# Two blocks of a feed-forward layer multiplied jointly by Strassen's products, and two attention blocks moved together, in a planned attention and feed-forward kernel

## The chip, the cores and the metric

The kernel runs on one core of a Trainium2 chip. The metric is device time in microseconds (us), the median of repeated executions. Engines are named as in the profile: PE (TensorE matmul), PEld (its weight loads), DVE (VectorE), ACT (ScalarE), POOL (GpSimd), SP (the queue that issues the DMAs).

## The reference

Kernelized attention, then a squared-ReLU feed-forward layer, then a normalized gated one, all in float32:

```python
def phi(x):                       # q, k: [4, 8, 576, 64], omega: [128, 64]
    proj = np.einsum('bhsd,md->bhsm', x, omega)
    h = proj - np.sum(x * x, axis=-1, keepdims=True) / 2.0
    return np.exp(h - np.max(h, axis=-1, keepdims=True)) / np.sqrt(m)
kv = np.einsum('bhsm,bhsd->bhmd', phi(k_s), v)
num = np.einsum('bhsm,bhmd->bhsd', phi(q_s), kv)
attn = num / (np.einsum('bhsm,bhm->bhs', phi(q_s), z)[..., None] + 1e-06)
...
h = np.maximum(x @ w_in, 0.0)     # x: [2304, 512], w_in: [512, 2048]
y = h * h @ w_out                 # w_out: [2048, 512]
...
xn = y / np.sqrt(np.mean(y * y, axis=-1, keepdims=True) + 1e-06) * rms_g
g = xn @ w_gate                   # w_gate, w_val: [512, 1536]
out = (g / (1 + np.exp(-g))) * (xn @ w_val) @ w_out2
```

## The kernel before

The 2304 tokens are cut into five blocks: block 0 to 3 hold 512 tokens of one batch element each, and a fifth, REM, holds the last 64 tokens of all four (256 columns). All matmuls of the two feed-forward layers are split in precision: each float32 operand becomes a high part (an ACT cast) and a low part (a DVE or POOL subtraction, helper `split`, L398), and a product is three matmuls (high by high, high by low, low by high), so that four 128-row pieces of the model dimension make 12 matmuls of 128x512.

`attention(b)` (L519) treats four pairs of heads of a block. A pair visits PE in small groups: features of k and of q (L577, 8 matmuls each), key-value sums (L635, L638), transposes (L686), numerators (L692, L697), transposes back (L722, L732). Between them DVE takes maxima and quotients and ACT the exponentials (L596). For block 2 and 3 (`long`) some of these groups are merged.

`moe1(j)` (L758) is the first feed-forward layer for one block: 16 chunks of 128 hidden units; `hpart` (L791, L804) makes a chunk's hidden tile h with 12 matmuls into a PSUM bank of class h, ACT takes the ReLU (L818) and the square (L820), and `ypart` (L826, L834) adds the chunk into four accumulators of class acc with another 12. Block 0 decodes the weights from their stored format and keeps part of them in SBUF (`wu`); the rest is written to DRAM and read again by each later block (`wr`). The second layer, `moe2` (L1126), takes blocks 0 and 1 together, then 2 and 3, and already uses seven products for eight (`seven`, L1057): for two chunks and two blocks 7 products of 6 matmuls, with DVE sums between them; its weight combinations are made beside the first layer by `make_units` (L918).

Nothing of this runs in the written order. Every operation becomes a node with an engine, a duration, a priority and its dependencies; `Plan.run` (L113) plays them through with those durations and buffer counts, and the order in which they start there is the order in which the instructions are issued, engine by engine. On the chip each engine then takes its instructions strictly in that order. The PSUM banks are divided by class: t (attention and others), h and acc, 2, 2 and 4 of eight. Early on, when PE has nothing to do in the plan, `fill` (L105) puts filler matmuls (L480, two of 128x256 on ones, into a spare bank) in its place, up to the planned time `FILL[1]`.

The calls before: `attention(0)`, then `attention(b + 1)` and `moe1(b)` for b = 0 to 3, so that attention 1 stands beside block 0, attention 2 beside block 1 and attention 3 beside block 2; then REM and `moe2` twice.

Of the kernel before, what the change touches and what calls it, by code (L numbers as in the profile page):

```python
# [9 lines left out]
F32 = mybir.dt.float32  # L10
# [28 lines left out]
class Node:  # L39
    __slots__ = ("eng", "dur", "fn", "prio", "idx", "tail", "alts", "deps", "ndeps", "outs", "bufs", "acq")  # L40


class Plan:
# [12 lines left out]
    FILL = (0.6, 45.0, 0.21)  # L56
# [11 lines left out]
    def add(self, eng, dur, prio, fn, r=(), w=(), after=(), tail=0.0, pre=(), alts=()):  # L68
        n = Node()
        n.alts = [(eng, dur, fn), *alts]  # L70
# [34 lines left out]
    def fill(self):  # L105
        n = Node()
        n.eng, n.dur, n.tail, n.prio, n.idx = "PE", self.FILL[2], 0.0, 0.0, -1
        n.bufs, n.acq, n.outs, n.deps, n.alts = [], [], [], set(), []
        b, f = self.filler
        n.fn = lambda: f(b.ap)  # L110
        return n

    def run(self):  # L113
# [15 lines left out]
        seq = 0  # L129

# [32 lines left out]
        while done < len(self.nodes):  # L163
# [4 lines left out]
            while events and events[0][0] <= now + 1e-9:  # L168
                _, _, kind, n = heapq.heappop(events)
                if kind == 0:  # L170
                    i = pick_alt(n)
                    heapq.heappush(ready[n.alts[i][0]], (n.prio, n.idx, i, n))
# [17 lines left out]
            for e in engs:  # L190
                if busy[e] > now + 1e-9:
                    continue
                held = []
                pick = None
                blocked = set()
                while ready[e]:
                    item = heapq.heappop(ready[e])
# [12 lines left out]
                    if ok:  # L210
                        for b, c, s in got:
                            slot[b] = (c, s)
                        pick = n
                        n.eng, n.dur, n.fn = n.alts[item[2]]
                        break
                    for b, c, s in got:
                        self.free[c].insert(0, s)
                    held.append(item)
                for it in held:
                    heapq.heappush(ready[e], it)  # L220
# [3 lines left out]
                if pick is not None:  # L224
# [3 lines left out]
                    if isinstance(pick.dur, Shared):  # L228
                        start = max(now, busy["POOL"])
                        held_by["DVE"] = start + pick.dur  # L230
                    busy[e] = start + pick.dur * (2.0 if e == "PE" and now < self.COLD else 1.0)
# [16 lines left out]
def kernel(  # L248
# [36 lines left out]
    LONG = 2  # L285
    SCALE = float(D) ** -0.25
# [9 lines left out]
    ph1_stack, att_stack = ExitStack(), ExitStack()  # L296
# [39 lines left out]
    plan.alloc["sm"] = slot_alloc("att", "sm", [P, 16], F32)  # L336
    plan.alloc["xa"] = slot_alloc("w2a", "xa", [P, 512], F32R)
# [18 lines left out]
    w1_d = [tc.dram_tile([P, 2, 512], F32, name=f"w1d{i}") for i in range(2 * C1)]  # L356

# [7 lines left out]
    b_w1d = [Buf(ap=t) for t in w1_d]  # L365

# [16 lines left out]
    def dma(prio, outap, inap, nbytes, r=(), w=(), after=()):  # L383
        return plan.add(
            "SP", nbytes / 311e3, prio,
            lambda: nc.sync.dma_start(out=outap(), in_=inap()), r, w, after, tail=2.0,
# [132 lines left out]
    def attention(b):  # L519
        base = (b - 1) * float(C1) if b else -25.0  # L520
        step = 3.7 if b else 6.0
        lead = base - (6.0 if b else 2.85)
        long = b >= LONG
        rem_x, rem_p = [], []
        ssr = Buf(["sm"])
# [8 lines left out]
        def operand(ldp, src, cls):  # L534

            x = Buf(["lt", cls])
            dma(ldp, lambda: x.ap, src, 262144, w=[x])
            return x

        def rem_prep(pr0):  # L540
            rem_x[:] = [operand(lead, lambda: rest_t[b].rearrange("p h n -> p (h n)"), "tr")]
            xr = Buf(["ld"], view=lambda t: t.rearrange("p h r d -> p (h r) d"))
            dma(lead, lambda: xr.ap, lambda: rest_r[b], 262144, w=[xr])
            row_norms(pr0, xr, ssr)
            dma(lead, lambda: vr_t[P - SR:], lambda: rest_v[b], 133120, w=[b_vr])

        def pair(hp):
# [7 lines left out]
            ld = pb - 3.0  # L555
            dma(ld + 0.1, lambda: vt, lambda: v_r[b, hp], 266240, w=[bv])
            stats = {}

            def transposed(nm, p0):
# [4 lines left out]
                dma(ld + 0.05, lambda: x.ap, lambda: src[b, hp].rearrange("p h r d -> p (h r) d"), 262144, w=[x])  # L564
# [3 lines left out]
            def features(p0, pbuf, x, places, ss, after=()):  # L568
# [10 lines left out]
                head = plan.add("PE", 0.24 * R + 0.2, p0, mm, [x, b_oms], fps, after, pre=[pbuf])  # L579
                mx = Buf(["sm"])  # L580
                for h, fp in enumerate(fps):
                    js = slice(*places[h])
                    plan.add("DVE", dve(M * R), p0 + 0.25 * u * h,
# [22 lines left out]
            features(pb + u, pk, xk, ODD, stats["k"], list(last_q))  # L606
# [5 lines left out]
            xq = transposed("q", pb + 2 * u)  # L612
            last_q[:] = [features(pb + 4 * u, pq, xq, ODD, stats["q"])]
# [17 lines left out]
            for h in range(2):  # L631
# [9 lines left out]
                if not long:  # L641
                    plan.add("PE", 0.13 * 5, pb + 3 * u + h * u, kv, [pk, pr, bv, b_vr, b_vz], [(kvp, h)],
                             kv_free)
            if long:
                plan.add("PE", 0.13 * 10 + 0.4, pb + 4 * u, kv2, [pk, pr, bv, b_vr, b_vz, b_const], [kvp], kv_free,
                         pre=[qrt])
# [5 lines left out]
            for hl in range(2):  # L652
                b_x[b, hl, hp] = Buf(["x"])
            xh, xl = b_x[b, 0, hp], b_x[b, 1, hp]
# [45 lines left out]
            for hs in ([(0, 1)] if long else [(0,), (1,)]):  # L700
# [9 lines left out]
                plan.add("PE", 0.44 * len(hs), pb + (6 + h0_) * u, trs, [pq] + [b_const],  # L710
                         [qps[h] for h in hs], pre=[qts[h] for h in hs])
                for h in hs:
                    copy(pb + (6.2 + h) * u, lambda h=h: qts[h].ap, lambda h=h: qps[h].ap, 512, [qps[h]], [qts[h]])
                plan.add("PE", 0.13 * R * len(hs) + (0 if h0_ else 0.36), pb + (7 + h1_) * u, mms,
                         [bkv] + [qts[h] for h in hs] + ([] if h0_ else [qrt]), [nps[h] for h in hs],
                         pre=[] if h0_ else [xw])
# [13 lines left out]
            def xtr():  # L730
# [27 lines left out]
    def moe1(j):  # L758
# [525 lines left out]
```

## Time and profile before

| what | value |
|---|---|
| median of 3 runs | 970.8 us (969.86 to 972.18) |
| profiled execution, its own time | 972.6 us |
| span, first to last instruction | 970.8 us |
| PE busy | 955.1 us (98%) |
| DVE, ACT, POOL busy | 688.4, 518.6, 78.8 us |
| granted TensorE clock, mean | 0.998 |

Span and busy times are those of the profiled execution. A matmul's record is longer than the step from one start to the next, since matmuls overlap; starts, not durations, give its cost. Matmuls on float32 tiles of the attention appear as two records each.

### The profile page before, as it was taken

What the parts mean: (1) busy time and instruction counts of PE and PEld (TensorE: products, weight loads), DVE (VectorE), ACT (ScalarE), POOL (GpSimd) and SP (SyncE); (2) the same over time, 40 slices, a digit from 0 to 9 for tenths busy, and PEclk for the clock granted to TensorE, in tenths of its full rate; (3) what the DMA queues carried; (4) which work ended last, traced back from release to release, by engine and by line L of the source; (5) the groups of instructions that cost most, each with busy time, mean ns of one, the idle gap of its engine ahead of it and who ended that gap; (6) DMA issues with size and microseconds to landing.
All of it is one profiled execution on the core that took longest, in us unless ns stands there. A gap on an engine that the chain in (4) does not pass through costs nothing.

```text
span 970.8 us, 16150 instructions
## 1 busy us (share of the span) xinstructions
PE 955.1 (98%) x6036; PEld 793.0 (82%) x6036; DVE 688.4 (71%) x1241; ACT 518.6 (53%) x1078; POOL 78.8 (8%) x69
## 2 busy tenths in 40 slices
PE   8999999999999999999999999999999999999998
PEld 7877777787888788788889888888878888888886
DVE  5889988756747556645745889989897757577573
ACT  6987788656446446445645658554443452323220
POOL 1123312000101010000100110000000000000000
PEclk9999999999999999999999999999999999999999
DMA  7878788888678565598978444324233221222203
GB/s 248 271 255 285 245 283 310 284 305 293 223 238 284 185 222 176 181 309 280 317 254 316 127 142 124 105 88 133 87 107 131 77 76 33 77 61 59 70 29 108
DMA packets 74845, 179.45 MB, mean 185 GB/s; under 512 B 8848, under 2 KB 12048, under 8 KB 74768
## 3 DMA queue, kind: packets, MB, share of 16 engines
q1 hardware_dynamic: 74768, 178.43, 56.0%
q8 instruction: 47, 0.77, 0.3%
q14 instruction: 30, 0.25, 0.1%
HBM read 143.27 MB, written 35.13 MB: 184 GB/s over the span
## 4 chain that ended last, share of the span: by engine, by line
PE 82%; DVE 8%; DMA 4%; ACT 3%; issue 1%; POOL 1%; SPq 0%; POOLq 0%; DVEq 0%; ACTq 0%
PE h L804 17%; PE acc L834 17%; PE acc L1046 12%; PE t L1107 11%; PE h L1046 11%; PE t L1046 4%; PE t L577 3%; DMA st<-in_w_gate_dram 1%; DMA ld<-in_k_r_dram 1%; PE t L692 1%; PE t L635 1%; DVE cc L1066 1%; PE acc L480 1%; PE t L686 1%; PE h L1107 1%
## 5 line engine op out<-in xcount | busy, mean ns | idle before, releaser
L834 PE MATMUL acc<-g,wr 128*128 128x512 f32 (+1 forms) x660 | 151.5, 373 | 1.2 <-POOL g L392 1.2
L804 PE MATMUL h<-x,wr 128*128 128x512 f32 x528 | 134.6, 398 | 0.0
L834 PEld LDWEIGHTS acc<-g,wr 128*128 128x128 f32 x660 | 113.4, 189 | 22.2 <-POOL g L392 1.4
L401 ACT CAST wq<-wq 128x512 fp32r<-128x512 f32 x108 | 66.5, 619 | 103.2 <-DMA wq<-w2d4g 15.8
L1107 PE MATMUL t<-wq,ub 128*128 128x512 f32 x474 | 116.7, 391 | 1.4 <-DVE oa L1115 1.3
L804 PEld LDWEIGHTS h<-x,wr 128*128 128x128 f32 x528 | 97.6, 189 | 21.7
L1046 PE MATMUL acc<-x,wq 128*128 128x512 f32 x324 | 106.9, 389 | 0.0
L1107 PEld LDWEIGHTS t<-wq,ub 128*128 128x128 f32 x474 | 88.4, 188 | 22.2 <-DVE oa L1115 2.9
L392 DVE TENSOR_TENSOR wq<-wq 128x512 fp32r<-128x512 f32 x108 | 79.7, 745 | 30.4 <-ACT wq L401 30.0
L818 ACT ACTIVATE f<-h 128x512 f32<-128x512 f32 (+1 forms) x80 | 44.9, 562 | 90.1 <-PE h L804 90.1
L1046 PE MATMUL h<-x,wq 128*128 128x512 f32 x252 | 85.3, 390 | 0.0
L392 DVE TENSOR_TENSOR g<-f,g 128x512 fp32r<-128x512 f32 (+1 forms) x61 | 39.6, 650 | 45.6 <-ACT f L499 34.5
L1046 PEld LDWEIGHTS acc<-x,wq 128*128 128x128 f32 x324 | 60.8, 188 | 12.8 <-DVE cc L1066 0.2
L1046 PE MATMUL acc<-xa,wq 128*128 128x512 f32 x192 | 69.8, 389 | 0.0
L834 PE MATMUL acc<-g,wu 128*128 128x512 f32 (+1 forms) x300 | 68.3, 373 | 0.0
L1066 DVE TENSOR_TENSOR cc<-acc,cc 128x512 f32<-128x512 f32 x84 | 57.8, 688 | 14.3 <-PE acc L1046 13.1
L1115 DVE TENSOR_TENSOR oa<-t,oa 128x512 f32<-128x512 f32 x75 | 50.9, 688 | 21.8 <-PE t L1107 21.3
L596 ACT ACTIVATE p<-t,sm 128x128 f32<-128x128 f32 x212 | 57.8, 382 | 14.2 <-DVE sm L589 12.2
L439 ACT ACTIVATE dw<-st 128x512 f32<-128x512 f32 x68 | 46.4, 692 | 29.2 <-DMA st<-in_w_out_dram 8.7
L804 PE MATMUL h<-x,wu 128*128 128x512 f32 x240 | 61.5, 399 | 0.0
L1046 PE MATMUL h<-xa,wq 128*128 128x512 f32 x168 | 60.5, 389 | 0.0
L834 PEld LDWEIGHTS acc<-g,wu 128*128 128x128 f32 x300 | 51.7, 189 | 9.6
(213 smaller groups left out, 1641.5 us busy)
## 6 DMA issues: line engine op xcount, KB each, us to landing
wr<-w1d SPq DMA_DIRECT2D x88, 512.0 KB, 4.6
st<-in_w_out_dram SPq DMA_DIRECT2D x28, 512.0 KB, 4.9
w1d<-wr SPq DMA_DIRECT2D x22, 512.0 KB, 4.3
st<-in_w_in_dram SPq DMA_DIRECT2D x16, 512.0 KB, 4.5
st<-in_w_gate_dram SPq DMA_DIRECT2D x12, 512.0 KB, 5.5
st<-in_w_val_dram SPq DMA_DIRECT2D x12, 512.0 KB, 5.2
st<-y SPq DMA_DIRECT2D x23, 256.0 KB, 4.2
v<-in_v_r_dram SPq DMA_DIRECT2D x16, 260.0 KB, 4.2
```

Source lines behind the costliest of these rows:

```text
L392: return lambda: en.tensor_tensor(out=lo(), in0=src(), in1=f32(hi()), op=ALU.subtract)
L401: first = plan.add("ACT", act(n), prio, lambda: nc.scalar.copy(out=hi(), in_=src()), rd, [whi], after, pre=[blo] if blo is not bhi else [])
L439: lambda: nc.scalar.activation(out=out(), in_=hf(), func=AF.Abs, scale=65536.0), [(st, 1)], [w])
L577: nc.tensor.matmul(fps[h].ap[:, i, :], lhsT=x.ap[ps, c], rhs=oms[ps, :], start=True, stop=True)
L596: nc.scalar.activation(out=pbuf.ap[:, j, :], in_=fp.ap[:, i, :], func=AF.Exp, bias=mx.ap[:, j:j + 1])
L804: nc.tensor.matmul(hb.ap[:, :n], lhsT=u.ap[:, wl, kk * P:(kk + 1) * P], rhs=xcols(j, xl, kk)(), start=(gi == 0 and ii == 0), stop=(gi == l ...
L818: lambda: nc.scalar.activation(out=rb.ap[:, :n], in_=hb.ap[:, :n], func=AF.Relu), [hb], [rb])
L834: nc.tensor.matmul(accs[e].ap[:, :n], lhsT=u.ap[:, w, es], rhs=x.ap[:, :n], start=(c == 0 and i == 0), stop=(c == C1 - 1 and i == 2))
L1046: nc.tensor.matmul(bank.ap[:, cols], lhsT=u.ap[:, wl, c0 + kk * P:c0 + (kk + 1) * P], rhs=x[kk][xl].ap[:, :cols.stop - cols.start], start= ...
L1066: lambda: nc.vector.tensor_tensor(out=out.ap, in0=bank.ap, in1=x.ap, op=ALU.add), [bank, x], [out])
L1107: nc.tensor.matmul(o.ap, lhsT=x[xl].ap[:, c0:c0 + P], rhs=us[f"o{i}"].ap[:, wl, :], start=i == n == 0, stop=i == 1 and n == 2)
L1115: lambda: nc.vector.tensor_tensor(out=oa.ap, in0=o.ap, in1=oa.ap, op=ALU.add), [o, oa], [oa])
```

## The change

Block 2 and 3 go through the first layer together (`moe1_pair`): the 16 chunks form eight pairs (c, c + 8). With `ALONE = 4`, pairs 0 to 3 are multiplied for block 2 alone, pairs 4 to 7 for both blocks by `seven`, then pairs 0 to 3 for block 3 alone; four of the eight pairs are joint. Attention 2 and 3 both stand beside block 1. New are: combinations of the raw weights (`sums`, to DRAM and back), combinations of the attention's results (`operands_pair`, with x of block 3 kept in DRAM), a third bank of class t for one of class h, priorities and planner constants, and a cost for changing between kinds of matmul in the planner.

```diff
-    FILL = (0.6, 45.0, 0.21)
+    SWITCH = 0.11
+    NEAR = 3.12
+    FILL = (0.6, 51.22, 0.21)
...
+                line = sorted(ready[e], key=lambda it: (it[0] - self.NEAR * (e == "PE" and mode > 0 and it[3].mode == mode), it[1]))
...
+    ALONE = 4
+    GATE = 8
+    PAIR = 2
+    HC = C1 // 2
+    ATT = ((-30.46, 5.32, 1.52), (-0.43, 3.33, 11.54), (C1 + -2.86, 1.49, 9.4), (C1 + 1.82, 1.29, 2.25))
...
-        "t": 2, "h": 2, "acc": 4,
+        "t": 3, "h": 1, "acc": 4,
...
-        base = (b - 1) * float(C1) if b else -25.0
-        step = 3.7 if b else 6.0
-        lead = base - (6.0 if b else 2.85)
+        base, step, lead = ATT[b]
+        lead = base - lead
...
+    def moe1_pair(ops, room):
...
+        def both(p, c):
+            pos = p - 2.99
+            u0 = unit(pos, c, 0)
+            ux, uy = (summed_unit(pos, c, k) for k in range(2))
+            ua = unit(pos, c + HC, 0, slice(256, 512))
+            w = {"A11": (u0, 0), "A12": (u0, 256), "S2": (ux, 0), "S3": (ux, 256), "S1": (uy, 0), "S4": (uy, 256),
+                 "A22": (ua, 256)}
+            r, nd = seven(p, w, ops, nodes[-2:-1] or [h_all[1, C1 - 1]], ["t", "h"], ["cs"], b_w1p)
+            nodes.append(nd)
+            used((u0, ux, uy, ua), nd)
+            return {k: squared(p + 0.02, r[i], i == 0) for i, k in enumerate(((0, 0), (0, 1), (1, 0), (1, 1)))}
...
+        work = [(c, 0) for c in range(ALONE)] + [(c, None) for c in range(ALONE, HC)] + [(c, 1) for c in range(ALONE)]
...
     attention(0)
-    for b in range(B):
-        if b + 1 < B:
-            attention(b + 1)
-        moe1(b)
...
+    attention(1)
+    moe1(0)
+    for b in range(PAIR, B):
+        attention(b)
+    moe1(1)
...
+    for c in range(ALONE, HC):
+        sums(c, C1 + 2.28 + 0.85 * (c - ALONE))
+    xp = operands_pair(PAIR * C1 + -29.26, ["xs", "x"], ["cs", "gs", "ys"])
+    hp_ = moe1_pair(xp, ["cs", "ys", "gs"])
```

On PE, block 2 before, one hidden tile takes 12 matmuls (x is the attention's result, wr the weights):

```order
L804 MATMUL h_3667<-x_1414,wr_3226 128x512
L804 MATMUL h_3667<-x_1736,wr_3226 128x512
L804 MATMUL h_3667<-x_2067,wr_3226 128x512
L804 MATMUL h_3667<-x_2422,wr_3226 128x512
L804 MATMUL h_3667<-x_1415,wr_3226 128x512
L804 MATMUL h_3667<-x_1737,wr_3226 128x512
L804 MATMUL h_3667<-x_2068,wr_3226 128x512
L804 MATMUL h_3667<-x_2423,wr_3226 128x512
L804 MATMUL h_3667<-x_1414,wr_3226 128x512
L804 MATMUL h_3667<-x_1736,wr_3226 128x512
L804 MATMUL h_3667<-x_2067,wr_3226 128x512
L804 MATMUL h_3667<-x_2422,wr_3226 128x512
```

On PE now, the first joint pair: two of its seven products, 6 matmuls each, into banks of class t (xs are combined operands):

```order
L1144 MATMUL t_4788<-x_2872,wu_1262 128x512
L1144 MATMUL t_4788<-x_3059,wu_1262 128x512
L1144 MATMUL t_4788<-x_2873,wu_1262 128x512
L1144 MATMUL t_4788<-x_3060,wu_1262 128x512
L1144 MATMUL t_4788<-x_2872,wu_1262 128x512
L1144 MATMUL t_4788<-x_3059,wu_1262 128x512
L1144 MATMUL t_4802<-xs_4597,wr_4576 128x512
L1144 MATMUL t_4802<-x_4649,wr_4576 128x512
L1144 MATMUL t_4802<-xs_4598,wr_4576 128x512
L1144 MATMUL t_4802<-x_4650,wr_4576 128x512
L1144 MATMUL t_4802<-xs_4597,wr_4576 128x512
L1144 MATMUL t_4802<-x_4649,wr_4576 128x512
```

Four hidden tiles (two chunks, two blocks) take 42 matmuls where they took 48.

On PE, at the end of attention 0, where the first chunk of block 0 begins, before (L480 are the fillers):

```order
L804 MATMUL h_884<-x_842,wr_767 128x512
L804 MATMUL h_884<-x_843,wr_767 128x512
L804 MATMUL h_884<-x_842,wr_767 128x512
L480 MATMUL acc_180<-ones 128x256 x2
L804 MATMUL h_926<-x_623,wu_894 128x512
L804 MATMUL h_926<-x_624,wu_894 128x512
L804 MATMUL h_926<-x_623,wu_894 128x512
```

The same place now (L501 are the fillers, L746 and L756 the last transposes of attention 0):

```order
L746 MATMUL t_998<-ident,xw_927 64x64 x2
L756 MATMUL acc_1004<-ident,xw_927 128x128 x4
L501 MATMUL acc_197<-ones 128x256 x24
L835 MATMUL h_838<-x_1005,wr_749 128x512
L835 MATMUL h_838<-x_1006,wr_749 128x512
L835 MATMUL h_838<-x_1005,wr_749 128x512
```

There are 102 filler matmuls in all where there were 82, and the last 24 stand in front of the first chunk's last piece.

On PE in block 1, now, numerators, key-value sums and a transpose of one attention stand in one group between matmuls of a chunk:

```order
L835 MATMUL h_4225<-x_2362,wr_3674 128x512
L716 MATMUL t_4234<-kv_83,qt_4163 64x65 x8
L721 MATMUL t_4234<-kv_83,qr_4000 64x65 x2
L716 MATMUL t_4235<-kv_83,qt_4164 64x65 x8
L656 MATMUL t_4258<-v_81,p_4182 64x65 x8
L659 MATMUL t_4258<-vr,pr_3287 64x65 x2
L656 MATMUL t_4258<-v_81,p_4182 64x65 x8
L659 MATMUL t_4258<-vr,pr_3287 64x65 x2
L642 MATMUL t_4258<-ident,pr_3287 128x64 x2
L835 MATMUL h_4225<-x_1403,wr_3674 128x512
```

Before, beside blocks 1 and 2, the numerators (L692) and the key-value sums (L635) stood in groups apart, with feed-forward matmuls between them. Over the whole program the stretches of feed-forward matmuls on PE fall from 83 to 79.

## Rows read from the trace of the kernel before

**Rows 1.** The page: busy time by engine; the chain that ended last, by engine.

```profile
PE 955.1 (98%) x6036; PEld 793.0 (82%) x6036; DVE 688.4 (71%) x1241; ACT 518.6 (53%) x1078; POOL 78.8 (8%) x69
...
PE 82%; DVE 8%; DMA 4%; ACT 3%; issue 1%; POOL 1%; SPq 0%; POOLq 0%; DVEq 0%; ACTq 0%
```

**Rows 2.** Windows by stage: length, busy us (instructions) of each engine, granted clock, DMA.

```profile
0.00:50.80 50.80, 47.70 (x615) 42.26 (x616) 37.87 (x100) 38.57 (x112) 5.90 (x12) 1.00 0.78 265
50.80:187.00 136.20, 131.34 (x965) 103.60 (x966) 117.36 (x234) 108.69 (x236) 32.63 (x23) 0.99 0.82 275
187.00:300.00 113.00, 112.39 (x861) 89.67 (x860) 73.43 (x159) 63.87 (x149) 5.89 (x7) 1.00 0.78 263
300.00:411.00 111.00, 111.00 (x859) 88.88 (x858) 66.36 (x148) 56.46 (x142) 9.00 (x7) 1.00 0.62 208
...
551.60:760.00 208.40, 207.74 (x937) 172.00 (x936) 184.08 (x291) 110.33 (x191) 7.01 (x5) 1.00 0.38 116
...
966.30:970.80 4.50, 0.00 (x0) 0.00 (x0) 0.67 (x1) 0.00 (x0) 0.00 (x0) 0.84 0.53 117
```

**Rows 3.** Who PE waited for: us in total, times, longest us.

```profile
PE t L577 <- ACT p L596: 2.4, 4, 0.8
PE t L1107 <- DVE oa L1115: 1.3, 5, 0.6
...
PE acc L834 <- POOL g L392: 1.2, 1, 1.2
PE t L635 <- ACT p L596: 1.1, 2, 0.9
```

**Rows 4.** PE in order of time, block 1: start us, us, line, tiles, count.

```profile
293.77 2.88 PE L804 MATMUL h<-x,wr 128*128 128x512 f32 x12
296.58 1.16 PE L577 MATMUL t<-oms,tt 64*128 64x128 f32 x16
297.67 3.02 PE L834 MATMUL acc<-g,wr 128*128 128x512 f32 x12
300.53 2.88 PE L804 MATMUL h<-x,wu 128*128 128x512 f32 x12
303.25 2.20 PE L834 MATMUL acc<-g,wr 128*128 128x512 f32 x9
```

**Rows 5.** PE in order of time, the start: fillers, and waits in brackets.

```profile
1.05 2.93 PE L480 MATMUL acc<-ones 128*128 128x256 f32 x12 [1.05 <-DVE ones L464]
...
14.60 2.66 PE L480 MATMUL acc<-ones 128*128 128x256 f32 x20
17.19 0.37 PE L577 MATMUL t<-oms,tt 64*128 64x128 f32 x1
```

**Rows 6.** Windows of 3 us after the last filler; the column before the last two is the clock.

```profile
50.00:53.00 3.00, 2.13 (x15) 1.38 (x13) 2.19 (x6) 2.99 (x7) 1.47 (x1) 1.00 0.93 297
53.00:56.00 3.00, 2.69 (x18) 2.26 (x19) 3.00 (x7) 1.62 (x3) 0.00 (x0) 0.77 0.89 347
56.00:59.00 3.00, 3.00 (x10) 2.32 (x10) 2.15 (x7) 2.32 (x5) 0.00 (x0) 0.66 0.87 271
```

**Rows 7.** DVE and POOL at 107 us, in order of time; DVE's sums of the second layer.

```profile
107.43 0.68 DVE L531 TENSOR_REDUCE sm<-ld 128x8 f32<-128x512 f32 x1
108.02 1.35 DVE L435 SCALAR_TENSOR_TENSOR st<-st 128x512 uint32<-128x512 uint32 x1
...
107.53 1.29 POOL L392 TENSOR_TENSOR wr<-dw,wr 128x512 fp32r<-128x512 f32 x1 [8.16 <-ACT wr L401]
...
L1066 DVE TENSOR_TENSOR cc<-acc,cc 128x512 f32<-128x512 f32 x84 | 57.8, 688 | 14.3 <-PE acc L1046 13.1
```

**Rows 8.** ACT's ReLU of one chunk, and PE around it.

```profile
312.09 0.63 ACT L818 ACTIVATE f<-h 128x512 f32<-128x512 f32 x1
...
310.01 2.20 PE L834 MATMUL acc<-g,wu 128*128 128x512 f32 x9
...
314.04 1.31 PE L804 MATMUL h<-x,wr 128*128 128x512 f32 x5
```

More of the change, by code (lines that the diff above doesn't have):

```diff
@@ L129, in run @@
         seq = 0
+        mode = 0
         def push(t, kind, n):
@@ L365 @@
     b_w1d = [Buf(ap=t) for t in w1_d]
+    b_w1s = {key: Buf(ap=t) for key, t in w1s_d.items()}
+    b_xd = Buf(ap=x_d)
+    raw = {}
     def f32(t):
@@ L385, in dma @@
             "SP", nbytes / 311e3, prio,
-            lambda: nc.sync.dma_start(out=outap(), in_=inap()), r, w, after, tail=2.0,
+            lambda: nc.sync.dma_start(out=outap(), in_=inap()), r, w, after, tail=2.5,
         )
@@ L812, in hpart @@
                 wb = [(u, parts[i][0]) for i, _ in group]
-                h_nodes[c] = plan.add("PE", pe(n, len(group)), base + c, mm, list(dict.fromkeys(wb + xb)), [hb])
+                h_nodes[c] = plan.add("PE", pe(n, len(group)), base + c + 0.2, mm, list(dict.fromkeys(wb + xb)), [hb],
+                                      [h_nodes[c - 1]] if j == REM and c else ())
             h_all[j, c] = h_nodes[c]
@@ L920, in make_units @@
             make_halves(c, ki, pos + ki)
-        for i in range(2):
-            store(pos + 2, (c, f"o{i}"), raw_unit(pos + 2, (w_out2, c + NC2 * i), last[-2:]))
+        for i, w in enumerate(two_raw(pos + 2, (w_out2, c), (w_out2, c + NC2))):
+            store(pos + 2, (c, f"o{i}"), w)
     def read_unit(c, nm, pos, gates):
@@ L938, with sums, part @@
     summed, held = [], []
+    begun = []
+    def sums(c, pos):
+        a, b = (Buf(["st"], view=lambda t: t.rearrange("p n t -> p (n t)").bitcast(F32).rearrange(
+            "p (t n) -> p t n", t=2)) for _ in range(2))
+        gates, begun[:] = begun[:] or last_split[:1], []
+        for t, cc in ((a, c), (b, c + HC)):
+            if kept(cc):
+                u, gate = w1[2 * cc], gates
+            else:
+                u, gate = t, []
+                dma(pos - 1.0, lambda t=t: t.ap, lambda cc=cc: w1_d[2 * cc], 524288, r=[b_w1d[2 * cc]], w=[t],
+                    after=gates)
+            begun.append(plan.add("DVE", Shared(dve(512)), pos, lambda t=t, u=u: nc.vector.tensor_tensor(
+                out=t.ap[:, 1, :], in0=f32(u.ap[:, 0, :]), in1=f32(u.ap[:, 1, :]), op=ALU.add), [u], [t], gate))
+        def part(t, k, i):
+            return lambda: t.ap[:, k, 256 * i:256 * i + 256]
+        for o, i, x, xi, xk, y, yi, yk, op in (
+                (b, 0, b, 0, 1, b, 1, 1, ALU.add),
+                (a, 1, a, 0, 1, b, 0, 1, ALU.subtract),
+                (a, 0, b, 0, 0, a, 0, 1, ALU.subtract),
+                (b, 1, a, 1, 1, a, 0, 0, ALU.subtract)):
+            both_sbuf(pos, part(o, 0, i), part(x, xk, xi), part(y, yk, yi), op, 256, [a, b], [o], False)
+        for k, t in enumerate((a, b)):
+            last.append(dma(pos, lambda k=k: w1s_d[c, k], lambda t=t: t.ap[:, 0, :], 262144, r=[t], w=[b_w1s[c, k]]))
     def rms(j, base, gates, cls, room, keep):
@@ L1055, with seven @@
     BANKS = ["h", "acc"]
-    def seven(prio, kind, us, ops, after):
-        a, b, d = Buf(BANKS), Buf(BANKS), Buf(BANKS)
-        s, u2, u3 = Buf(["cc"]), Buf(["cc"]), Buf(["cc"])
-        w0, w1_, w2_ = us[kind + "0"], us[kind + "1"], us[kind + "2"]
-        k4 = "gv".index(kind)
+    def seven(prio, w, ops, after, banks, cls, opened):
+        a, b, d = Buf(banks), Buf(banks), Buf(banks)
+        s, u2, u3 = Buf(cls), Buf(cls), Buf(cls)
         def plus(bank, x, out):
@@ L1202 @@
     plan.add("NONE", 0.0, 0.0, open_w2b, w=[b_w2b], after=ph1_nodes)
-    sets = [read_units(c, E1 + (c - 1.0 if c else -7.0), held[:2]) for c in range(NC2)]
+    sets = [read_units(c, E1 + (c - 0.48 if c else -1.99), held[:2]) for c in range(NC2)]
     hidden0 = moe2(0, sets, x01, None)
```

293 lines of the change are left out of this document (228 added, 65 removed), and 1 row of the table slots.

## The prediction

> **What bounds the kernel now.** I read the page first. PE is busy 955.1 of 970.8 us, the next engine, DVE, 71% [rows 1]. The chain that ended last is 82% PE [rows 1], and the rest of it lies mostly at the start and beside block 0. The windows by stage say where the missing 15.7 us are [rows 2]: 3.1 in the first 50.8 us, 4.9 from there to 187 us (block 0 with attention 1), 0.6 and 0.0 beside blocks 1 and 2, 4.5 after the last matmul. So from 187 us on PE's own work is the time, and what matters is how many matmuls it has and how far apart they start. The waits that exist are few [rows 3]: for the exponentials p (2.4 and 1.1 us), for the low part of REM's last chunk on POOL (1.2), for the row sums of the second layer (1.3).
>
> The price of a matmul is read from starts [rows 4]: 12 matmuls begin at 300.53 and the next group at 303.25, so 2.72 us or 0.227 each. The same rows show what an attention group costs beyond itself: the 12 ahead of the features take 2.81 (293.77 to 296.58) and the 12 behind them 2.86 (297.67 to 300.53), 0.23 us in all more than 2.72 each.
>
> **The change, part by part.**
>
> Products. A joint pair has 42 matmuls where it had 48. The loop makes four pairs joint (pairs 4 to 7), so 24 matmuls of 128x512 go, which the order confirms: 5028 without fillers before, 5004 now. 24 by 0.227 is **5.4 us off** the engine that sets the time.
>
> Attention groups. 83 stretches of feed-forward matmuls become 79; four interruptions by 0.23 [rows 4] are **0.9 us off**. The attention's own matmuls are the same.
>
> The start. 20 more fillers, two of them among the first 14, which run slow (12 in 2.93 us, 0.24 each), the others at 2.59 us for 20 (14.60 to 17.19), 0.13 each [rows 5]: 18 by 0.13 and 2 by 0.24 are 2.8 us. Fillers cost nothing if PE would have waited there anyway, and 2.8 if it wouldn't. By the order the useful work ahead of the last filler is the same in both (80 key-value, 72 numerator and 32 transpose matmuls in each; 9 feed-forward matmuls fewer, one group of features and a few transposes more), so I take **2.8 us on**. Against it: behind the last filler of before, from 50 to 56 us, PE idles 0.87 + 0.31 us, and the granted clock falls from 2.4 to 1.2 GHz for a while (means 0.77 and 0.66 over 53 to 59 us), which costs 3 by 0.23 and 3 by 0.34, 1.7 us [rows 6]. Now 24 fillers stand exactly there, so PE is not idle before the first long stretch: I take **1.2 and 1.7 us off**. The start comes out even, with 0 to -2.9 if the fillers fill what was waiting, and +2.8 if the fall of the clock and the idling only move.
>
> The Trainium skill, "TensorE: Matmul & The Clock Gate", section "What's actually happening", says that the low clock is the default and that activity releases it; by that rule steady fillers keep the 1.7 us. Rows 6 agree as far as they go: the fall comes right after the row in which PE is busy least. If fillers did not count as activity, the 1.7 us would stay in the time.
>
> DVE, ACT, POOL. By the order DVE has 98 more instructions (1243 to 1341), ACT 13, POOL 13, mostly 128x512. At DVE's 0.69 us [rows 7] that is 68 us. It lies beside PE: the blocks 1 to REM (187 to 551.6 us) hold 220 us of DVE work in 365 us now, and would hold 288 in about 358, or 80%. Beside the second layer DVE is busy 184.1 of 208.4 us, 88%, and PE misses 0.7 us there [rows 2], with the same `seven`. So this is **nothing**, as long as no stage goes above what that one shows. The joint stretch is the densest: I count 124 DVE instructions by 364 matmuls, some 77 us in 83, 93%. If the cover is gone there, the price is what PE saves in that stretch, 5.4 us.
>
> The Trainium skill, "SBUF — State Buffer", section "SBUF: two separate sides", says that DVE with two SBUF inputs and a POOL instruction shut each other out for a whole instruction. Rows 7 agree: at 108.02 a DVE instruction takes 1.35 us beside POOL's. By that rule each of 13 more POOL instructions can cost DVE about 0.7 us, 9 us in all, which PE would see only where DVE is the bound.
>
> DMA and SP. 523 issues become 542. 13 reads of 512 KB go, and three half reads, 8 stores and 8 loads of combined weights, 5 reads for the sums and x of block 3 come; the bytes are about the same, and block 0 (share 0.82 [rows 2]) loses none and gains next to none. Nothing.
>
> One bank of class h instead of two. A chunk's first matmul now waits until the ReLU of the chunk before has read the bank. In the latest case I found, h ends by 310.2 us, ACT is done at 312.72, and the next h begins at 314.04 [rows 8]; the accumulation between them, 12 by 0.227, always covers 2.72 us of it. So nothing, and at most some tenths of a us where ACT is late. The third bank of class t goes the other way: the features (two banks each) wait for the exponentials that still hold t, 3.5 us in all [rows 3], and could stop waiting. Between 0 and 3.5 off I take 0, since the attention pairs now come faster.
>
> Two attentions beside block 1. The stage of block 1 has 384 matmuls of the layer (16 chunks by 24), 87 us by 0.227; of its 113 us [rows 2] the other 26 are attention 2. With attention 3 it would be 139 us. By the order I count 100 us of DVE work there, 72%, less than the 117.4 of 136.2 us beside block 0 [rows 2]. The wait that could come is the third rival.
>
> Sum: -5.4 - 0.9 + 2.8 - 1.2 - 1.7 = -6.4 us against the execution's own 972.6, or 966.2. That execution was 1.8 us above the median of 970.8, so the median after is **964.5 us**.
>
> **The rivals.**
>
> *The start keeps its loss.* The fillers delay PE, and idling and the low clock come a little later all the same: +2.9, 967.4 us. For it: the planner sets fillers by planned, not real, idleness. Against: the gap they now stand in is the real one.
>
> *The third bank frees the features.* The 3.5 us of waits for p [rows 3] go as well: 961.0 us. For it: nearly all waits of the middle are of this one kind. Against: ACT and DVE beside block 0 are at 80% and 86% [rows 2], and a bank doesn't make them faster.
>
> *The joint stretch is bound by DVE.* The 5.4 us are saved on PE and waited for DVE: 969.9 us, no change that can be measured. From: DVE above 82 us in that stretch; POOL's collisions [rows 7] work towards it. Against: 88% with no wait in the second layer.
>
> *Slower: attention waits beside block 1.* Attention 1 beside block 0 makes PE wait 4.9 us for four pairs [rows 2], 1.2 per pair, nearly all for exponentials and features. With a pair of heads every 17 us (139 by 8) instead of 28 (113 by 4), the eight pairs of attention 2 and 3 could wait as much: 9.7, less the 0.6 that blocks 1 and 2 wait now, is +9.1, or 973.6 us. It decides from 6.3 by 8, about 0.8 us per pair. For it: the pairs follow closely and PE takes its instructions in order. Against: what makes block 0 wait is the decoding of the weights on DVE and ACT, which is not there in block 1.
>
> **How the numbers follow.** 0.2% (1.9 us) is about what a measurement of this kernel can tell from no change. The forecast gets 0.43, the start 0.15, the third bank 0.16, DVE 0.13, the waits 0.13. The first three are faster by over 0.2% (0.74), DVE is the same (0.13), the waits are slower (0.13). The range goes from 957.5 (the third bank's 961.0 with the start's -2.9 and a little more) to 972.5, which leaves out the worse part of the waits and what nobody foresees; the forecast's own range is 961 to 968.
>
> **What would show it.** Products: 24 matmuls fewer, and the joint pairs at 0.227 us per matmul with no wait inside `seven`. Start: a clock of 1.00 and less than 0.5 us of idle time on PE from 50 to 60 us, and about 1.2 + 1.7 us less lost there than the fillers add. Waits: PE's idle time beside block 1 under 2 us. DVE: under 90% in the joint stretch. The prediction is wrong if PE idles more than 6 us between 187 us and the second layer, or if matmuls there start farther apart than 0.227 us.

## The result, and the profile after

The changed kernel takes 960.4 us (median of 4 runs, 958.6 to 961.7) beside 971.5 for the kernel before: ratio 0.9886, 95% interval 0.9863 to 0.9909, or 11.1 us less. The forecast was 6.3 less (964.5). Sign and range (957.5 to 972.5) hold; the size does not, and the time lies just outside the 961 to 968 that the forecast gave itself. The profiled execution took 961.7 us, span 959.8.

The page's busy times and the chain by engine, as in [rows 1]:

```profile
PE 946.5 (99%) x6032; PEld 787.8 (82%) x6032; DVE 734.7 (77%) x1339; ACT 521.0 (54%) x1091; POOL 95.7 (10%) x82
...
PE 84%; DVE 7%; DMA 4%; ACT 3%; issue 1%; SPq 1%; POOL 0%; DVEq 0%; ACTq 0%; POOLq 0%
```

Windows, columns as in [rows 2]: start, block 0 with attention 1, block 1 with attention 2 and 3, the joint pairs, the first part of the second layer; then the three windows of [rows 6].

```profile
0.00:54.00 54.00, 48.46 (x647) 43.09 (x648) 42.54 (x107) 38.01 (x115) 10.74 (x16) 1.00 0.81 270
54.00:187.00 133.00, 132.34 (x1043) 103.62 (x1043) 118.77 (x242) 113.57 (x257) 35.03 (x24) 1.00 0.87 285
185.00:316.90 131.90, 131.68 (x1231) 105.60 (x1230) 91.17 (x221) 76.04 (x200) 8.94 (x8) 1.00 0.75 256
355.60:437.40 81.80, 80.76 (x354) 65.88 (x353) 70.54 (x117) 48.04 (x82) 4.52 (x4) 1.00 0.73 244
542.30:759.80 217.50, 217.10 (x980) 179.72 (x979) 184.39 (x290) 110.73 (x191) 8.93 (x6) 1.00 0.39 112
...
50.00:53.00 3.00, 3.00 (x34) 2.81 (x31) 3.00 (x7) 1.37 (x3) 0.20 (x1) 1.00 0.72 226
53.00:56.00 3.00, 3.00 (x30) 2.47 (x29) 3.00 (x9) 2.23 (x8) 0.00 (x0) 1.00 0.78 222
56.00:59.00 3.00, 3.00 (x13) 2.26 (x13) 2.69 (x5) 2.63 (x8) 1.35 (x2) 1.00 0.88 277
```

PE lacks (is not busy for) 0.7 us beside block 0, 0.2 beside block 1, 1.0 in the joint stretch, and the clock stays at 2.4 GHz where it fell before. From 54 to 187 us, the kernel before lacks 3.7:

```profile
54.00:187.00 133.00, 129.32 (x949) 102.12 (x946) 114.97 (x228) 106.32 (x230) 31.16 (x22) 0.99 0.82 274
```

PE's waits in the changed kernel, as in [rows 3]:

```profile
PE t L598 <- ACT p L617: 1.4, 2, 1.2
...
PE t L1144 <- DVE cs L1162: 0.9, 2, 0.5
...
PE t L1339 <- DVE oa L1347: 0.3, 1, 0.3
...
PE acc L866 <- POOL g L413: 0.2, 1, 0.2
```

PE in order of time: a joint pair, where 24 matmuls start in 5.44 us (366.48 to 371.92), 0.227 each; and the two places where `seven` waited.

```profile
366.48 1.52 PE L1144 MATMUL t<-xs,wr 128*128 128x512 f32 x6
367.84 2.88 PE L1144 MATMUL t<-x,wr 128*128 128x512 f32 x12
370.56 1.52 PE L1144 MATMUL t<-xs,wr 128*128 128x512 f32 x6
371.92 5.60 PE L1265 MATMUL acc<-g,wr 128*128 128x512 f32 x24
...
404.82 1.66 PE L1144 MATMUL t<-x,wr 128*128 128x512 f32 x6 [0.50 <-DVE cs L1162]
406.83 1.41 PE L1144 MATMUL t<-xs,wr 128*128 128x512 f32 x5 [0.36 <-DVE cs L1162]
```

Where the 11.0 us between the two spans come from, summed over each matmul's start to the next one's start in the two traces (a wait counts with the matmul ahead of it):

| PE's time by kind, us | before | after | difference |
|---|---|---|---|
| fillers (82, now 102) | 15.1 | 17.9 | +2.8 |
| attention features (576) | 46.9 | 43.8 | -3.1 |
| first layer's matmuls without REM's hidden tiles, with four for row sums (1732, now 1708) | 394.9 | 386.1 | -8.8 |
| all else ahead of the second layer | 94.4 | 94.4 | 0 |
| second layer, first to last start | 414.5 | 412.3 | -2.2 |
| after the last start | 5.0 | 5.3 | +0.3 |

Where in time this lies is told by the loss: the time that has passed at a point of PE's order, less what the matmuls done by then (fillers left out) take at 0.227 us per 128x512, 0.120 per 128x256 and the attention's mean steps beside blocks 1 and 2 of before. Fillers, waits, visits and the low clock all count as loss.

| loss, us | before | after | difference | after, run again |
|---|---|---|---|---|
| to 70 us | 24.2 | 25.0 | +0.8 | 24.6 |
| 70 to 187 us | 9.8 | 6.9 | -2.9 | 6.5 |
| 187 us to REM | 10.5 | 8.7 | -1.8 | 8.8 |
| REM | 1.4 | 1.7 | +0.3 | 1.7 |
| second layer | 3.4 | 1.2 | -2.2 | 1.9 |
| after the last start | 5.0 | 5.3 | +0.3 | 5.2 |

With the 24 matmuls' 5.4 these differences make the 11.0. The low clock of before, nine steps from 54.4 us on that take 1.7 us too long, is gone whole. Of the features' 3.1, 1.7 lie ahead of 60 us, at the start, and only 1.4 beside block 0. The forecast had nothing for 70 to 187 us and nothing for the second layer.

### The profile page after: what moved, and what is told of

Same layout as the page of the kernel before. It is cut to its first block, busy times and chain, and to the rows that moved or that the text cites. A ratio compares the mean times of both kernels' runs of the same rounds, so it can differ in the third digit from the quotient of the medians.

```text
span 959.8 us, 16323 instructions
## 1 busy us (share of the span) xinstructions
PE 946.5 (99%) x6032; PEld 787.8 (82%) x6032; DVE 734.7 (77%) x1339; ACT 521.0 (54%) x1091; POOL 95.7 (10%) x82
## 4 chain that ended last, share of the span: by engine, by line
PE 84%; DVE 7%; DMA 4%; ACT 3%; issue 1%; SPq 1%; POOL 0%; DVEq 0%; ACTq 0%; POOLq 0%
PE acc L1144 16%; PE t L1339 13%; PE h L835 10%; PE acc L866 10%; PE h L1144 7%; PE t L1144 5%; PE t L1265 4%; PE t L598 3%; PE acc L1265 3%; PE h L1245 3%; PE t L1245 2%; PE t L656 1%; PE t L716 1%; PE t L710 1%; DMA st<-in_w_out_dram 1%
## 5 line engine op out<-in xcount | busy, mean ns | idle before, releaser
L1144 PE MATMUL acc<-x,wq 128*128 128x512 f32 x432 | 146.5, 389 | 0.0
L1144 PE MATMUL acc<-xa,wq 128*128 128x512 f32 x252 | 98.0, 389 | 0.0
L866 PE MATMUL acc<-g,wr 128*128 128x512 f32 (+1 forms) x396 | 86.8, 362 | 1.0 <-DVE g L413 0.8
L866 PEld LDWEIGHTS acc<-g,wr 128*128 128x128 f32 x396 | 64.6, 189 | 12.9 <-DVE g L413 1.6
L835 PE MATMUL h<-x,wr 128*128 128x512 f32 x264 | 69.3, 400 | 0.8 <-DVE sm L694 0.8
L835 PEld LDWEIGHTS h<-x,wr 128*128 128x128 f32 x264 | 47.7, 188 | 11.4 <-issue 0.9
L1144 PEld LDWEIGHTS acc<-xa,wq 128*128 128x128 f32 x252 | 47.3, 188 | 9.8
L605 DVE TENSOR_REDUCE sm<-t 128x4 f32<-128x512 f32 x61 | 40.9, 684 | 15.9 <-PE t L598 15.8
L422 ACT CAST ub<-cc 128x512 fp32r<-128x512 f32 x45 | 27.9, 621 | 44.6 <-DVE cc L1323 37.9
L1144 PE MATMUL h<-x,wq 128*128 128x512 f32 x144 | 46.4, 390 | 0.0
L465 DVE SCALAR_TENSOR_TENSOR dw<-dw,st 128x512 uint32<-128x512 uint32 x61 | 43.4, 711 | 1.3 <-ACT st L454 1.0
```

The costliest lines, as they stand in the source:

```text
L422: first = plan.add("ACT", act(n), prio, lambda: nc.scalar.copy(out=hi(), in_=src()), rd, [whi], after, pre=[blo] if blo is not bhi else [])
L465: lambda: nc.vector.scalar_tensor_tensor(out=out().bitcast(U32), in0=out().bitcast(U32), scalar=3, in1=half(st.ap, 0), op0=ALU.logical_shi ...
L835: nc.tensor.matmul(hb.ap[:, :n], lhsT=u.ap[:, wl, kk * P:(kk + 1) * P], rhs=xcols(j, xl, kk)(), start=(gi == 0 and ii == 0), stop=(gi == l ...
L866: nc.tensor.matmul(accs[e].ap[:, :n], lhsT=u.ap[:, w, es], rhs=x.ap[:, :n], start=(c == 0 and i == 0), stop=(c == C1 - 1 and i == 2))
L1144: nc.tensor.matmul(bank.ap[:, cols], lhsT=u.ap[:, wl, c0 + kk * P:c0 + (kk + 1) * P], rhs=x[kk][xl].ap[:, :cols.stop - cols.start], start= ...
```

## The experiments

Times are medians; ratios are to the kernel before on the same chip, with 95% intervals. The changed kernel is the yardstick: 960.4, ratio 0.9886.

| run | us | ratio | interval |
|---|---|---|---|
| third bank alone, on before | 978.7 | 1.0076 | 1.0054 to 1.0099 |
| two banks of t again | 993.3 | 1.0227 | 1.0210 to 1.0243 |
| no joint pair | 970.8 | 0.9983 | 0.9967 to 0.9999 |
| fillers to 45.0 | 961.6 | 0.9889 | 0.9867 to 0.9910 |
| five joint pairs | 975.6 | 1.0043 | 1.0031 to 1.0055 |
| no grouping | 975.9 | 1.0048 | 1.0032 to 1.0064 |
| old attention priorities | 969.3 | 0.9977 | 0.9964 to 0.9990 |
| old second-layer priorities | 972.5 | 1.0020 | 1.0007 to 1.0034 |
| landing time 2.5, on before | 983.4 | 1.0128 | 1.0108 to 1.0149 |
| landing time 2.0, on after | 976.9 | 1.0062 | 1.0042 to 1.0082 |
| five pairs, other dates | 963.5 | 0.9919 | 0.9898 to 0.9940 |
| the changed kernel again | 961.4 | 0.9896 | 0.9879 to 0.9913 |

### The third bank alone

```diff
 # kernel before
-        "t": 2, "h": 2, "acc": 4,
+        "t": 3, "h": 1, "acc": 4,
```

> The kernel before with three banks of class t and one of class h, nothing else. Theory (the third bank frees the features and the second layer): the waits for p go (3.5 us before) and those for oa in the second layer too (the second layer became 2.2 us shorter in the changed kernel), so 4 to 6 us less than before, ratio 0.994 to 0.996; the planner puts in 10 more fillers, which may give back up to 1.3. Rival (the priorities did it, a bank makes no engine faster): only the second layer's 2.2 us, ratio about 0.998, and beside block 0 PE still idles as in rows 2.

7.1 us slower than before; both expectations miss. Who PE waited for in this kernel (the first four rows of that view):

```profile
PE h L804 <- ACT f L818: 4.5, 4, 2.2
PE t L1107 <- DVE oa L1115: 2.5, 5, 1.8
PE t L577 <- ACT p L596: 2.2, 2, 1.6
PE acc L834 <- POOL g L392: 1.9, 2, 1.2
```

The waits for p fall, beside block 0 (54 to 187 us) to 1.6 us from 3.5; those 1.6 are one wait, at 54.57 us. But the single bank of h costs 4.5 us of waiting for the ReLU in the old order, and the waits for oa are not removed. The bank alone, in the order that the planner makes with it, is no gain.

### Two banks of t again

```diff
 # changed kernel
-        "t": 3, "h": 1, "acc": 4,
+        "t": 2, "h": 2, "acc": 4,
```

> The changed kernel with two banks each of t and h. Theory (third bank): 4 to 6 us above the changed kernel, 964.5 to 966.5, with the waits for p and for oa back. Rival (priorities): only the second layer's 2.2 us, about 962.5. The planner puts in 18 fillers fewer here (84 for 102), worth up to 2.3 us less.

33 us slower, far outside both. Two views, the waits from 357 to 460 us and windows of 10 us:

```profile
PE t L756 <- DVE xw L695: 4.2, 1, 4.2
PE t L1144 <- ACT xs L422: 4.1, 1, 4.1
PE t L1144 <- ACT x L422: 2.8, 1, 2.8
```

```profile
370.00:380.00 10.00, 4.62 (x54) 3.16 (x50) 5.20 (x15) 4.61 (x12) 0.00 (x0) 0.97 0.87 313
380.00:390.00 10.00, 4.42 (x14) 2.83 (x14) 8.61 (x16) 5.47 (x11) 2.11 (x2) 0.67 0.41 117
390.00:400.00 10.00, 6.78 (x14) 4.13 (x15) 10.00 (x18) 5.09 (x10) 0.00 (x0) 0.51 0.43 163
```

With two banks attention 3 isn't done beside block 1; its last transposes (L756) stand among the first joint products, whose operands xs and x follow from them. PE is idle for 14.2 of 30 us there and the clock falls to 1.2 GHz. In this plan the third bank is what lets two attentions go beside one block; without it the slower rival of the prediction comes true, one stage later. The waits for p beside block 0 are 1.8 us here.

### No joint pair

```diff
-    ALONE = 4
+    ALONE = 8
```

> The changed kernel with ALONE = 8: no pair is joint, blocks 2 and 3 go one after the other in the new order. 24 matmuls of 128x512 more. Theory (products are worth their matmuls): 24 by 0.227, so 5.4 us above the changed kernel, 965.9, with PE's steps of 0.227 in the stretch as in the changed kernel. Rival (the joint stretch also saves what the separate chunks lose to single ReLU and bank waits): above 7 us. Other rival (waits on DVE inside the joint stretch eat part): under 4 us.

10.4 us above the changed kernel, in runs that spread from 965.3 to 973.9. In the profiled execution (972.9) the first layer's matmuls without REM's hidden tiles take 392.9 us for 1732, 6.8 more than the changed kernel's 386.1 for 1708: 5.4 are the 24 matmuls, the rest are longer steps, the waits for POOL in REM among them. PE in order of time at the end of REM:

```profile
541.40 1.60 PE L835 MATMUL h<-xr,wr 128*128 128x256 f32 x12
542.84 0.28 PE L866 MATMUL acc<-g,wu 128*128 128x256 f32 x1
545.33 2.33 PE L866 MATMUL acc<-g,wu 128*128 128x256 f32 x11 [2.22 <-POOL g L413]
547.46 2.38 PE L835 MATMUL h<-xr,wr 128*128 128x256 f32 x12
```

After 2.2 us of waiting for POOL, 12 matmuls take 2.21 us (547.46 to 549.67) instead of 1.44: the clock's mean is 0.64 from 545 to 548. REM's hidden tiles cost 25.7 us here for 23.0, REM as a whole 59.0 for 51.9, and the features, whose code is the same, 46.5 for 43.8. So the products save their matmuls, and no-joint also loses at REM, which the edit doesn't touch. But a part of the 5.4 goes again: from the last attention matmul to REM the loss is 2.2 us in the changed kernel (2.9 when run again) and 0.5 here, so the joint stretch keeps some 3 to 3.7 of the 5.4. That is the expectation's other rival, in its mechanism; the total hides it.

### Fillers to the planned 45.0

```diff
-    FILL = (0.6, 51.22, 0.21)
+    FILL = (0.6, 45.0, 0.21)
```

> The changed kernel with fillers only up to the planned 45.0 us as before: 68 fillers for 102. Theory (fillers cost what they save): 34 fillers by 0.13 are 4.4 us less PE work, against idling of 1.2 and the fall of the clock of 1.7 us that come back: between 1.5 less and no change, with a window of clock under 1.00 between 45 and 60 us. Rival (fillers fill time that would be idle anyway): 1.5 to 3 us more than the changed kernel. Other rival (the clock stays up without them): 3 to 4 us less.

961.6, the same within the interval: the first theory. Windows of 3 us where the 34 fillers are missing:

```profile
50.00:53.00 3.00, 1.57 (x7) 0.78 (x5) 3.00 (x9) 1.31 (x4) 0.00 (x0) 0.90 0.87 308
53.00:56.00 3.00, 3.00 (x19) 2.29 (x17) 3.00 (x7) 3.00 (x11) 0.00 (x0) 0.50 0.55 174
56.00:59.00 3.00, 3.00 (x8) 2.42 (x8) 3.00 (x6) 2.21 (x4) 2.44 (x2) 0.50 0.60 225
```

The idling and 1.2 GHz come back without them, as in [rows 6], and cost about what the fillers cost. The Trainium skill, "TensorE: Matmul & The Clock Gate", section "What's actually happening", has the low clock as the default that activity releases; the two kernels agree, 0.50 without and 1.00 with the fillers from 53 to 56 us.

### Five joint pairs

```diff
-    ALONE = 4
+    ALONE = 3
```

> The changed kernel with ALONE = 3: five joint pairs instead of four, 6 matmuls fewer (3170 of 128x512 for 3176), the start word for word the same. Theory (a joint pair is worth its matmuls and DVE has room): 1.4 us less than the changed kernel, so 0.9872 of before. Rival (more joint work makes PE wait for DVE): no change, or up to 2 us more, with new waits for cs in the joint stretch.

15 us slower than the changed kernel. Neither theory: REM begins at 486.44 us, 3.95 earlier than in the changed kernel, so the blocks did gain (1.4 us of it by the six matmuls fewer). All is lost behind that. PE's waits in the second layer:

```profile
PE h L1144 <- ACT x L422: 6.1, 1, 6.1
PE h L1144 <- ACT cc L1165: 1.6, 1, 1.6
PE h L1144 <- DVE x L413: 0.6, 1, 0.6
```

The second layer's first operands (x) are late. In REM DVE still decodes weights for the units until 521 us, and scales the first of those operands (L1050) at 529.34, 43 us into REM; in the changed kernel at 507.88, 17 us into it. From 511 to 529 us DVE is idle for most of the time. SP issues the loads of y, from which those operands are made, at 523.33 us, behind the store of a decoded unit (w2d5o) that waited 6.5 us for DVE; in the changed kernel they go out at 501.16. So the preparation work ahead of them in SP's order makes them late.

### No grouping of attention matmuls in the plan

```diff
-    SWITCH = 0.11
-    NEAR = 3.12
+    SWITCH = 0.0
+    NEAR = 0.0
```

> The changed kernel with NEAR = 0 and SWITCH = 0: the planner no longer keeps attention matmuls of a kind together (118 fillers for 102). Theory (the grouping is small): about 0.9 us more for the visits and up to 2 for the fillers, 961 to 963. Rival (the grouping is what took the waits from the stretch beside block 0): 3 us or more above the changed kernel, with PE idle there over 3 us.

15 us slower, but not where the rival put it: PE lacks 1.1 us from 54 to 187, and REM begins at 491.35, 1.0 later, the size that the visits were given (with 16 more fillers). REM and the second layer then take 56.3 and 419.0 us for 51.9 and 412.3, with waits for operands (xa) and cc. Up to REM grouping is small; most of the 15 us is lost behind it.

### Old attention priorities

```diff
-    ATT = ((-30.46, 5.32, 1.52), (-0.43, 3.33, 11.54), ...
+    ATT = ((-25.0, 6.0, 2.85), (0.0, 3.7, 6.0), ...
-            features(pb + 1.98 * u, pk, xk, ODD, stats["k"], list(last_q))
+            features(pb + u, pk, xk, ODD, stats["k"], list(last_q))
...
```

> The changed kernel with the priorities of before inside a pair of attention heads, and with the start, step and lead of before for attention 0 and 1; the third bank, the joint pairs and the places of attention 2 and 3 stay. Theory (the third bank took the waits from beside block 0): within 1.5 us of the changed kernel, PE idle 54 to 185 us under 2 us. Rival (the new priorities did): 3 us or more above it, with PE idle beside block 0 near the 4.9 of rows 2.

PE lacks 1.1 us from 54 to 187, against 3.7 in the kernel before and 0.7 in the changed one, and waits 0.3 there for the exponentials. So with the rest of the change in place the old priorities bring little of the waiting back, and two banks (1.8 us of waits) more. The total is another matter, 8.9 above the changed kernel by the medians. The profiled execution is the fastest of its twelve (965.0) and shows only 3.3 of it, 2.2 ahead of block 2; the rest stays open.

### Old second-layer priorities

```diff
-    sets = [read_units(c, E1 + (c - 0.48 if c else -1.99), held[:2]) for c in range(NC2)]
+    sets = [read_units(c, E1 + (c - 1.0 if c else -7.0), held[:2]) for c in range(NC2)]
...
-    rv23 = [rms(j, G0[0] + j - 0.69, ...
+    rv23 = [rms(j, G0[0] + j - 0.3, ...
```

> The changed kernel with the old priorities in the second layer alone (the loads of its weights, and the operands of its second half); all that stands ahead of it is unchanged. Theory (those priorities shortened the second layer, since the third bank alone didn't): 2.2 us more, and the short waits for oa at steps of 39 us back. Rival (the stages ahead leave the engines in another order): no change, second layer at 412 us.

12 us slower, and the short waits for oa did not come back, so these priorities did not remove them. The second layer still takes 417.3 us for 412.3, with one wait of 2.8 for an operand (xa), so the rival misses too. The loads of the second layer now come earlier and their casts get in front of REM's ReLU: ACT casts wq and xa from 524.83 us on and takes the ReLU only at 528.79. PE's waits in REM:

```profile
PE h L835 <- ACT f L850: 3.3, 2, 2.8
PE acc L866 <- POOL g L413: 1.4, 1, 1.4
```

REM takes 58.9 us for 51.9: with one bank of h a ReLU that comes late makes PE wait.

### The planned landing time of a transfer, both ways

In the second layer DVE's order is the same in every kernel with the change, and another in before and in the third bank alone. One planner number decides it, which the prediction passed over:

```diff
 # kernel before
-            lambda: nc.sync.dma_start(out=outap(), in_=inap()), r, w, after, tail=2.0,
+            lambda: nc.sync.dma_start(out=outap(), in_=inap()), r, w, after, tail=2.5,
```

> The kernel before with one number of the planner changed, the landing time that it plans for a transfer, 2.5 us instead of 2.0 (one of the constants that the change brings). DVE then takes the sums of the second layer in the order of the changed kernel. Theory (this order shortened the second layer): it takes about 412.3 us instead of 414.5, without the waits for oa at steps of 39 us. What the same number does to the stages ahead is open; if nothing, the total is 2.2 us less, ratio 0.998. Rival (the third bank or the new priorities shortened it): still 414.5.

> The changed kernel with the planned landing time of a transfer back at 2.0 us. DVE takes the second layer's sums in the order of before. Theory (this order): the second layer takes 2.2 us more than the changed kernel's 412.3, with the short waits for oa back, and the total is at least that much above 960.4. Rival (bank or priorities): 412.3 stays.

At one kind of place the order does what the theory says, both ways: at the four places 39 us apart the steps lose 0.45 us each in before (from 820 us) and 0.1 each with 2.5; the changed kernel has no such step after 720 us, and with 2.0 they lose 0.45 again. The totals and the second layer's time don't follow: with 2.5 the kernel before is 13 us slower, since the first operand x comes 6.8 us late and the second layer takes 425.4; with 2.0 the changed kernel is 16.5 us slower, its second layer 419.7 with 4.5 us of waits for oa, one of them 3.8. DVE and POOL in the kernel before, in order of time, at the first of the four places:

```profile
816.06 1.78 DVE L392 TENSOR_TENSOR wq<-wq 128x512 fp32r<-128x512 f32 x1
817.76 0.68 DVE L1066 TENSOR_TENSOR cc<-acc,cc 128x512 f32<-128x512 f32 x1
...
819.56 1.28 DVE L1115 TENSOR_TENSOR oa<-t,oa 128x512 f32<-128x512 f32 x2
...
816.00 1.29 POOL L392 TENSOR_TENSOR ub<-cc,ub 128x512 fp32r<-128x512 f32 x1 [37.13 <-ACT ub L401]
```

And in the changed kernel:

```profile
807.33 0.69 DVE L413 TENSOR_TENSOR wq<-wq 128x512 fp32r<-128x512 f32 x1
807.93 0.68 DVE L1162 TENSOR_TENSOR cc<-acc,cc 128x512 f32<-128x512 f32 x1
808.53 0.68 DVE L1347 TENSOR_TENSOR oa<-t,oa 128x512 f32<-128x512 f32 x1
...
807.54 1.63 POOL L413 TENSOR_TENSOR ub<-cc,ub 128x512 fp32r<-128x512 f32 x1 [36.79 <-ACT ub L422]
```

Before, POOL starts 0.06 us ahead of wq, and wq takes 1.78 us instead of 0.69; the sums oa come late by that, and PE with them. Now wq starts first, POOL takes the longer (1.63 for 1.29), and the two DVE instructions that read a PSUM bank (acc, t) run in 0.68 beside it. The Trainium skill, "SBUF — State Buffer", section "SBUF: two separate sides", says that whichever starts first of a POOL instruction and a DVE one with two SBUF inputs holds the shared ports to its end. The Trainium skill, "SBUF — State Buffer", section "Who interferes with whom", says that a DVE instruction with at most one SBUF input, outside the two-port modes, doesn't contend with POOL. The rows agree with both: 1.78 us behind POOL's start and 0.69 ahead of it, 0.68 for those that read PSUM.

### Five pairs, other dates

The same ALONE = 3, with dates in the plan moved for the combinations, loads, unit preparation and second-layer operands, for example:

```diff
-            pos = p - 2.99
+            pos = p - 0.82
...
-        make_units(c, PAIR * C1 + -3.73 + 4.35 * c)
+        make_units(c, PAIR * C1 + -5.64 + 4.41 * c)
```

> Five joint pairs (ALONE = 3) with the planned dates of the combinations, the loads, the unit preparation and the second layer's operands moved. Theory (with four dates unchanged five pairs lost only because the operands of the second layer came late behind more preparation work): no wait for x at the start of the second layer, and a time from 1.4 us below to 1 us above the changed kernel, ratio 0.987 to 0.9895 of before. Rival (five joint pairs are more than DVE can feed): above 0.995, with waits in the joint stretch.

963.5 instead of 975.6, and no wait for x: the first theory by its mechanism, though 0.9919 lies just above its bound. From the last attention matmul to REM the loss is 0.3 us, for 2.2 in the changed kernel: DVE can feed five pairs, and the changed kernel's waits inside `seven` come from its order. From the first matmul of block 2 to the second layer it is 2.4 us faster than the changed kernel (223.0 for 225.4); it loses more in the second layer, 416.6 for 412.3. By the medians no version here beats the changed kernel.

### The changed kernel again

> The changed kernel once more, beside the others on one chip. 960.4 us within 1.5, ratio 0.9865 to 0.991; the second layer 412.3 us again, PE idle under 1.5 us from 54 to 187 us.

961.4, as expected; the second layer 413.0 us, PE's lack from 54 to 187 us 0.8, the features 44.6 us, the waits inside `seven` 1.8 us for 0.9. So the changed kernel's own executions differ by 0.7 to 0.9 us in such terms. The features' row holds the wait for the transfer tr at the start, 0.8 us in before and in the changed kernel's first execution and 3.4 here, so its 3.1 us are no measure of the waits for p; the lack from 54 to 187 us is.

## Why the prediction was right, and what it lacked

**Products, -5.4: right in the matmuls.** 24 fewer in the traces (1732 to 1708), the joint pairs at 0.227, and they come back when the products are undone. "No wait inside `seven`" was too strict: 0.9 us, and 1.8 when run again. With the longer steps around these waits the joint stretch loses 1.7 to 2.4 us more than separate chunks do, which the forecast did not take off; with five pairs and other dates it loses 0.3.

**Attention visits, -0.9: too much, at this price.** The steps into attention that hold no wait cost 0.066 us each beyond 0.227 before and 0.067 now, so four visits fewer are 0.3; the part behind a visit was not told apart.

**The start, even: right, but not term by term.** The loss to 70 us grew by 0.8 (0.4 when run again). The clock gave back the 1.7, and PE lacks nothing from 50 to 59 us; but over the first 54 us it is idle 5.5 us for 4.3 before, so that idling only moved. The fillers' row grew by the 2.8 with waits in it, and by 1.3 when run again. Taking the fillers away changes nothing in the total. The rival that the start keeps its loss, +2.9, falls.

**The third bank, taken at 0: the step that failed.** The prediction gave it 0 to 3.5 us "and could stop waiting", and chose 0 "since the attention pairs now come faster". PE's lack from 54 to 187 us fell from 3.7 to 0.7 us. The argument "a bank doesn't make them faster" was the wrong question: ACT and DVE at 80% and 86% were not the limit, for in the changed kernel they are busy 85% and 89% of that stretch and PE waits less. The waits for p in that stretch, by who waited (features read no p, so they wait for a bank that an exponential still reads; the key-value sums read p themselves):

| kernel | PE's lack | at features | at key-value sums, transposes |
|---|---|---|---|
| before | 3.7 | 2.4 | 1.1 |
| third bank alone | 1.9 | 1.6 | 0 |
| two banks again (new priorities) | 2.2 | 0.3 | 1.5 |
| old attention priorities (three banks) | 1.1 | 0 | 0.3 |
| changed | 0.7 | 0.2 | 0 |

Undone by itself in the changed kernel, the bank brings back 1.5 us of the lack and the priorities 0.4; the bank alone on the kernel before leaves 1.6 of the 3.5 us of waits for p, and the rest of the change without the bank 1.8. So the bank is shown to be a large part of the 3.0 us, not all of it, and each edit also makes the planner choose another order. That rival's 961.0 is the nearest to the measured time, in part by luck: the second layer's 2.2 is not in it.

**One bank of h, nothing: right only in this order.** PE waits for no ReLU in the changed kernel; with the order of before one bank costs 4.5 us, and with the old second-layer priorities 3.3.

**The second layer, not in the sum: -2.2.** The prediction treated it as unchanged because its code is. Its order isn't: one planned landing time moves DVE's sums against POOL's subtractions, at four places worth 0.45 us each. That these 1.8 us are most of the 2.2 is read from the two traces; no run here got the 2.2 by that number alone.

**DVE, 93% estimated in the joint stretch:** 70.5 of 81.8 us, 86%; its rival falls as priced, though the waits for cs there are for DVE. The 98 more instructions took 46 us of DVE in all, not 68. **Attention beside block 1:** 0.2 us of waiting, but only with the third bank; without it the slower rival comes true, behind block 1.

The sum with the measured terms: products -5.4, start +0.8, 70 to 187 us -2.9, 187 us to REM beside the products -1.8, REM +0.3, second layer -2.2, end +0.3, together -11.0 (before rounding), where the forecast had -5.4, -0.1, 0, -0.9 (the visits), 0, 0 and 0. So the waits beside block 0 were mis-sized by 2.9 us and the second layer by 2.2; the stretch from 187 us to REM adds 0.9 and the start, REM and the end take 1.5 back.

Open: why 12 runs with the old attention priorities spread by 6 us, which edits beside the third bank took the rest of the waits for p, and which steps from 187 us to REM became shorter. That the undone versions lose at the border of REM and the second layer is shown where a trace has the wait there (five pairs, no grouping, old second-layer priorities, 2.5 on before); for the medians as a whole it is only argued.

## What to carry to other kernels

Where a planner sets the order, a constant that nobody costs (a planned landing time) reorders stages whose code is unchanged, so the border between two stages, where the next one's first operands must be ready, is to be read before and after each change. A wait for a result can be a wait for the buffer that it occupies: a third buffer can then help although no engine is faster, if the buffer given up elsewhere has slack in that order. Undoing one part of a tuned order measures that part and all that it makes late, so the trace of its stage counts, not the total.

## What the runs showed of the hardware

Two executions of the same changed kernel waited 0.8 and 3.4 us at the start for the same transfer (tr), and yet their last matmuls start at 954.56 and 954.58 us. After a wait of 2.2 us (no joint pair), and after 3 us in which PE was busy for 1.57 (fillers to 45.0), the granted clock fell to 1.2 GHz for some microseconds; behind the first of these, 12 matmuls took 2.21 us instead of 1.44, so that the wait cost more than its length. A DVE instruction of 0.69 us with two SBUF inputs took 1.78 where POOL's had started 0.06 us ahead of it.
